# A tuned attention and MLP kernel on one core: small vectors spread on chip, first K and Q columns loaded apart, and the instruction order searched anew

## The chip, the cores and the metric

The kernel runs on one core of a Trainium2 chip. The metric is the device time of one execution in microseconds (us). The core has five engines that run side by side: TensorE (PE; PEld is its weight load), VectorE (DVE), ScalarE (ACT), GpSimd (POOL) and SyncE (SP, which here only issues DMAs). Sixteen DMA engines move data between HBM and on-chip memory.

## The reference, cut to what matters

```python
g = sigmoid((x * gate_w).sum(-1, keepdims=True))      # x: 2048 tokens x 512
a = A(x, wq, wk, wv, wo, beta)   # 32 heads of 16, four segments of 512 tokens:
                                 # causal softmax attention in a segment, plus a memory
                                 # (phi(q) M / phi(q) z) of the segments before,
                                 # mixed per head by sigmoid(beta)
b = (gelu(x @ w_gate) * (x @ w_up)) @ w_down          # 512 -> 1792 -> 512
return g * a + (1 - g) * b
```

Two inputs are tiny: `beta` has 32 values and `gate_w` has 512, all bfloat16.

## The kernel before

The kernel describes its work as tasks with estimated durations and lets a list scheduler, run at build time, put them in order on each engine. A table `BIAS` of priorities, found by search, steers the list. Every engine then executes its list strictly in order.

A segment's attention is a rhythm of 20 steps: TensorE computes scores (lines L730) into four banks of PSUM, ScalarE takes one exponential over 2048 columns (L738), GpSimd masks it (L750), TensorE multiplies by V (L763). In the gaps between scores TensorE does projections and MLP matmuls (L421). The four score banks exist once, so scores n+1 cannot start before exponential n has read scores n.

The head of the kernel, with the parts that changed:

```python
for a in range(2):                                   # x of segment 0, 2 x 256 KB, natural layout
    dma(f"x0_{a}", SP, ..., A_x[0, a * 256:(a + 1) * 256, :] ...)
wdma("wk", SP, wk[:], r4(A_wk), 524288)
wdma("wq", SP, wq[:], r4(A_wq), 524288)
wdma("wv", SP, wv[:], r4(A_wv), 524288)
wdma("beta", ACT, betab[:], A_beta.partition_broadcast(P), 8192)
for g in range(4):                                   # beta again, in another layout
    bsrc = A_beta.rearrange("(t g j) -> g t j", g=4, j=2)[g]
    dma(f"betaT{g}", ACT, lambda g=g: betaT[32 * g:32 * g + 32, :].rearrange("p (t j) -> p t j", j=2),
        lambda bsrc=bsrc: bsrc.partition_broadcast(32), ...)
wdma("gatew", ACT, gatew[:], gate_w.rearrange("(kb p) -> p kb", p=P), 1024, nonc=True)
# ... w_gate, x of segment 1 (DMA transposes), w_up, w_down, wo, all on SP
# warm-up: 10 matmuls on zeros; then x0 is transposed by TensorE in four groups, each into one
# of three work banks of PSUM and copied out from there; then 3 more warming matmuls ("warmE")
```

`partition_broadcast(32)` makes 32 partitions read the same source bytes. So each of the four `betaT` loads is 128 reads of 4 bytes. `betab` is 128 reads of 64 bytes. `gatew` is 512 reads of 2 bytes.

The softmax here doesn't subtract the row's maximum and nothing guards it: scores larger than these inputs give would overflow.

Of the kernel before, what the change touches and what calls it, by code (L numbers as in the profile page):

```python
# [10 lines left out]
BF = mybir.dt.bfloat16  # L11
# [18 lines left out]
BIAS = {  # L30
    "D1": 28, "D2": -81, "D3": -30, "G1": -23, "G2": -26, "G3": 129, "GdT0": 14, "GdT1": 24, "GdT3": -43,
    "Gev1": 11, "K0": 2, "K2": -15, "K3": -12, "Q0": -31, "Q1": 2, "Q2": -21, "Q3": -15, "U0": 55, "U1": 21,
    "U2": -32, "U3": 1, "Um1": 8, "Um2": 42, "Um3": 4, "V1": 13, "V2": -15, "Vev0": -8, "Vev2": 2, "Vev3": 28,
    "den1": -8, "den3": 4, "denp2": 4, "exp1": 4, "exp2": -2, "exsT0": -30, "exsT1": -8, "exsT2": 4, "exsT3":
    -12, "fin1": -20, "fin2": -15, "fin3": -64, "gate2": -4, "gelu1": -8, "gelu2": 13, "gelu3": -6, "gexs0":
    -34, "gexs2": 30, "gts0": -4, "gts2": -28, "gts3": -73, "kp0": 39, "kp1": -9, "kp2": 94, "kp3": 30,
    "msk1": -40, "msk2": 7, "msk3": 6, "mz0": 4, "mz1": 22, "mz2": -64, "mzacc0": 23, "mzacc2": -2, "mzbd0":
    9, "mzbd1": -6, "mzbd2": -19, "norm1": -6, "norm2": -33, "num1": -9, "num3": 10, "nump1": 22, "nump2": 34,
    "nump3": 2, "oTd2": -26, "pkT1": 4, "pkc0": 30, "pkc1": -43, "pke0": -35, "pke2": 4, "pqc2": -8, "pqc3":
    8, "pqe1": -4, "pv0": 21, "pv1": -23, "pvt2": -11, "pvt3": -52, "qk0": 26, "qk3": -12, "x2": 4, "x3": -37  # L40
}
# [68 lines left out]
class Sched:  # L110
# [32 lines left out]
    def schedule(self):  # L143
# [26 lines left out]
        for t in tasks:  # L170
            if npred[t.id] == 0:
                for e in t.alts:
                    ready[e].add(t)
        cur = {e: 0.0 for e in ENGINES}
        bank_free = {b: 0.0 for b in range(self.nbanks)}
# [3 lines left out]
        while len(order) < n:  # L179
# [33 lines left out]
            if t.nbytes:  # L213
                dma_free = max(t.finish + 1.5, dma_free) + t.nbytes / DMA_RATE
                avail = dma_free
# [111 lines left out]
def mm_t(n):  # L327
    return max(0.026, n / 2370.0)
# [19 lines left out]
def _build(es, nc, A_x, A_wq, A_wk, A_wv, A_wo, A_beta, B_w_gate, B_w_up, B_w_down, gate_w, out):  # L348
    def sb(name, shape, dtype=BF):
        return es.enter_context(nc.sbuf_tensor(name, shape, dtype))  # L350
# [30 lines left out]
    exsT = [sb(f"exsT{i}", [P, 16], F32) for i in range(2)]  # L381
    betaT = sb("betaT", [P, 8])
    gexpT = sb("gexpT", [P, 8], F32)
    omgT = sb("omgT", [P, 8], F32)
# [56 lines left out]

    def dma(name, eng, out_ap, in_ap, reads, writes, nbytes, issue=0.7, transpose=False, bias=0.0, sm=None,
            nonc=False):
        sm = sm if sm is not None else sem("d")

        def f(e):
            if transpose:
                return e.dma_start_transpose(out_ap(), in_ap())
            if nonc:
                with nc.allow_non_contiguous_dma(reason="small vector"):  # L450
                    return e.dma_start(out_ap(), in_ap())
            return e.dma_start(out_ap(), in_ap())  # L452
        return task(name, eng, [Instr(f, reads, writes, issue, dma_sem=sm)], bias=bias, nbytes=nbytes)
# [7 lines left out]
    def xdma(s):  # L461
# [12 lines left out]
    task("ident", POOL, [  # L474
        Instr(lambda e: e.memset(ident[:], 0.0), writes=[("c", "ident")], est=0.2),
        Instr(lambda e: e.affine_select(out=ident[:], in_=ident[:], compare_op=ALU.not_equal, fill=1.0, base=0,
# [6 lines left out]
    for a in range(2):  # L483
# [3 lines left out]
            [("hT", 1, 2 * a), ("hT", 1, 2 * a + 1)], 262144, bias=rank[0], issue=0.45)  # L487
    wdma("wk", SP, wk[:], r4(A_wk), 524288)
    wdma("wq", SP, wq[:], r4(A_wq), 524288)
    wdma("wv", SP, wv[:], r4(A_wv), 524288)  # L490
    wdma("beta", ACT, betab[:], A_beta.partition_broadcast(P), 8192)
    for g in range(4):
        bsrc = A_beta.rearrange("(t g j) -> g t j", g=4, j=2)[g]
        rank[0] -= 20.0
        dma(f"betaT{g}", ACT, lambda g=g: betaT[32 * g:32 * g + 32, :].rearrange("p (t j) -> p t j", j=2),
            lambda bsrc=bsrc: bsrc.partition_broadcast(32), [], [("betaT", g)], 1024, nonc=True, bias=rank[0],
            issue=0.5)
    wdma("gatew", ACT, gatew[:], gate_w.rearrange("(kb p) -> p kb", p=P), 1024, nonc=True)
    wdma(("wg", 0), SP, wg[:, :, 0:half], wgr[:, :, 0:half], 917504)
# [8 lines left out]
                             [("P",)], 0.43)], bias=5001.0)  # L508
    for i in range(9):
        gw = Grp(banks)  # L510
        task(f"warm{i}", PE, [Instr(lambda e, gw=gw: e.matmul(gw.f32()[:, :], warm[:, 0:128], warm, start=True,
                                                              stop=True), [wkey], [gw.key], 0.43)],
             grp=gw, bias=5000.0 - i)
    for kb in range(4):
        g = Grp(banks)
        task(f"x0t{kb}", PE, [Instr(lambda e, g=g, kb=kb, a=a: e.transpose(
            g.bf()[:, a * 128:(a + 1) * 128], xin[:, a, kb * 128:(kb + 1) * 128], ident[:, :]),
            [("hT", 1, a), ("c", "ident")], [g.key], mm_t(128)) for a in range(4)], grp=g)
        copy_out(f"x0ev{kb}", g, lambda kb=kb: xT[0][:, kb, :], lambda g=g: g.bf()[:, 0:512], [g.key],
                 [("xT", 0, kb)], 512)  # L520
    task("warmE", PE, [Instr(lambda e: e.matmul(Pb[:, :], warm[:, 0:128], warm, start=True, stop=True), [wkey],
                             [("P",)], 0.3) for _ in range(3)], bias=4.0,
         after=[t for t in S.tasks if t.name == "x0t3"])

    c = [Instr(lambda e: e.memset(maskc[0][:], 0.0), writes=[("c", "mask", 0)], est=0.1)]
# [23 lines left out]
    def exp_task(phase, name, instrs, **kw):  # L549
# [4 lines left out]
        if phase > 0 and name.endswith("_0A0"):  # L554
# [3 lines left out]

    exp_task(0, "gexp", [
        Instr(lambda e: e.activation(gexp[:], betab[:], ACTF.Exp), [("w", "beta")], [("c", "gexp")], 0.25),  # L560
        Instr(lambda e: e.activation(gexpT[:], betaT[:], ACTF.Exp), [("betaT", g) for g in range(4)],
              [("c", "gexpT")], 0.25)])
    task("gmat", DVE, [
        Instr(lambda e: e.tensor_scalar(gexpT[:], gexpT[:], 1.0, None, ALU.add), [("c", "gexpT")],
              [("c", "gexpT")], 0.2),
        Instr(lambda e: e.reciprocal(omgT[:], gexpT[:]), [("c", "gexpT")], [("c", "omgT")], 0.2),
        Instr(lambda e: e.tensor_scalar(gtmp[:], gexp[:], 1.0, None, ALU.add), [("c", "gexp")], [("c", "gtmp")], 0.2),
        Instr(lambda e: e.reciprocal(gtmp[:], gtmp[:]), [("c", "gtmp")], [("c", "gtmp")], 0.2),
        Instr(lambda e: e.tensor_tensor(gmat[:], gexp[:], gtmp[:], ALU.mult), [("c", "gexp"), ("c", "gtmp")],
              [("c", "gmat")], 0.2)])  # L570

    def proj_T(name, s, t, w, wkey, dst, wkeys, even=None):

        g = Grp(banks)
        xs = xT[s % NX]
        pieces(name, g, [mm(g, lambda: g.f32()[:, :], w[:, kb, t * 128:(t + 1) * 128], xs[:, kb, :],
                            [("xT", s % NX, kb), ("w", wkey)], kb == 0, kb == 3, 512) for kb in range(4)], 2)
        if even is not None:
            task(name + "even", ACT, [Instr(lambda e: e.activation(even[0], g.f32()[:, :], ACTF.Copy,
                                                                   scale=maskc[0][:, 0:1]),  # L580
                                            [g.key, ("c", "mask", 0)], [even[1]], act_t(512, ap=True))], grp=g)
        copy_out(name + "ev", g, lambda: dst[:, t, :], lambda: g.f32()[:, :], [g.key], wkeys, 512)

    def phi_task(nm, s, phase, src, skey, dst, dkey, i):
# [12 lines left out]
            Instr(lambda e: e.tensor_tensor(dst[:, t0:t1, :], dst[:, t0:t1, :], ex[:], ALU.add),  # L597
                  dk + [("pex", i)], dk, dve_t(1024, 2))])

    def prep(s):  # L600
# [19 lines left out]
        for tile in range(4):  # L620
# [24 lines left out]
        cross = task(f"exsT{s}", POOL, [Instr(lambda e, g=g, c=c: e.tensor_copy(  # L645
            exsT[sl][32 * g:32 * g + 32, c:16:4], exs[32 * c:32 * c + 32, s4]), [("exs", s), ek], [ek], 0.2)
            for g in range(4) for c in range(4)])
        for ins in cross.alts[POOL]:
# [3 lines left out]
            exsT[sl][:].rearrange("p (o b) -> p o b", o=1).to_broadcast([P, 8, 16]), ALU.mult),  # L652
            [ek, ("c", "omgT")], [("GdT", sl)], 0.3)])
        if s > 0:
            for i in range(2):
# [9 lines left out]
                      0.3),  # L665
                Instr(lambda e: e.reciprocal(nf, nf), [("nd",)], [("nd",)], 0.3),
                Instr(lambda e: e.tensor_tensor(ndsc[:], ndsc[:], Gm[sl][:], ALU.mult), [("nd",), ("Gm", sl)],
# [230 lines left out]
    fins = []  # L898
    sem_out = [sem("so") for _ in range(16)]
    prep(0)  # L900
    memory(0)
# [99 lines left out]
```

## Time and profile before

| | us |
|---|---|
| time, median of 3 runs | 293.34 (293.33 to 293.64) |
| span of the profiled run | 290.8 |
| head: start to first scores | 16.13 |
| middle: first scores to last scores | 260.27 |
| tail: last scores to end | 14.42 |

"First scores" is the start of the first L730 matmul in the timeline. Head, middle and tail, cut at the score matmuls, add up to the span.

The page of the kernel before, first its totals, then forty slices of the span (busy tenths, granted clock in tenths, DMA throughput), then one DMA queue and the chain of waits:

```profile
PE 272.3 (94%) x2150; PEld 114.2 (39%) x2189; DVE 191.3 (66%) x332; ACT 217.5 (75%) x172; POOL 103.0 (35%) x193
...
PE   6699999999999899996799999999999999999995
...
PEclk9899999999999999999799999999999999999999
...
GB/s 88 285 246 342 280 102 2 0 1 2 0 2 72 73 109 38 1 0 20 54 2 0 36 38 36 10 29 2 0 2 0 1 3 0 48 45 38 19 2 72
...
q10 hardware_dynamic: 1248, 0.01, 0.2%
...
PE 79%; DVE 9%; ACT 5%; DMA 3%; issue 2%; POOL 1%; SPq 0%; ACTq 0%
```

TensorE is the engine that bounds: 94% busy, 79% of the chain. But its first two slices (14.5 us) are only 6 tenths busy, and those are warming matmuls in good part; the clock is below full in the second; and in the first slice the DMA engines move 88 GB/s, against 342 later. Queue q10 (the one that ScalarE issues on) carries 1,248 packets for 0.01 MB.

The chain of waits, in order of time (start, length, what):

```profile
2.33 9.81 DMA wq<-in_A_wq_dram
...
12.19 3.17 PE psW L421 x7
```

The windows view of the head (window, its length, busy time and count for PE, PEld, DVE, ACT and POOL, then the granted clock, DMA share, GB/s):

```profile
2.00:4.00 2.00, 2.00 (x6) 0.76 (x5) 0.00 (x0) 0.00 (x0) 1.85 (x4) 1.00 0.38 103
4.00:6.00 2.00, 1.73 (x7) 0.55 (x4) 0.00 (x0) 0.54 (x1) 2.00 (x2) 1.00 0.38 124
12.00:14.00 2.00, 1.81 (x5) 0.71 (x6) 0.80 (x4) 0.96 (x2) 0.00 (x0) 0.55 0.88 282
14.00:16.00 2.00, 2.00 (x7) 0.51 (x5) 0.95 (x2) 0.19 (x1) 0.00 (x0) 0.59 1.07 389
```

About 113 GB/s move from 2 to 6 us, with the DMA engines 38% busy. The clock falls to 0.55 and 0.59 between 12 and 16 us.

The worst place of the middle, in the timeline of TensorE (start, length, instruction, in brackets the idle time before it and what ended it):

```profile
134.64 0.40 PE L730 MATMUL psXALL<-qT,kpad_1 32*128 32x256 bf16 x8 [0.19 <-ACT pt L738]
135.24 0.41 PE L421 MATMUL psW<-mzbd,phq 128*128 128x128 bf16 x4 [0.20 <-DVE otok L677]
137.16 0.39 PE L730 MATMUL psXALL<-qT,kpad_1 32*128 32x512 bf16 x4 [1.51 <-ACT pt L738]
139.61 2.34 PE L421 MATMUL psW<-xT,wu 128*128 128x512 bf16 x5 [2.05 <-DVE otok L677]
```

Here the only matmuls in TensorE's list between two scores are a few small ones (`mzbd,phq`, the memory's numerator), and the next projection waits 2.05 us until VectorE has written `otok` and so freed one of the three work banks.

### The profile page before, as it was taken

How to read it: one execution, taken by the hardware profiler on the slowest of the kernel's cores; microseconds unless marked ns; L12 is line 12 of the kernel's file. 1: busy time of each engine (PE TensorE's matmuls, PEld its weight loads, DVE VectorE, ACT ScalarE, POOL GpSimd, SP SyncE). 2: the span in 40 equal slices, each digit the busy share in tenths (PEclk: the TensorE clock that was granted, in tenths of full speed). 3: DMA queues.
4: the chain of work that ended last, by engine and by line, in shares of the span. 5: the costliest groups of instructions: out<-in, count | busy, mean ns of one | idle time of the engine just before them, and what ended most of it. 6: DMA issues, size and time to landing. Idle time of an engine off the chain costs nothing.

```text
span 290.8 us, 5337 instructions
## 1 busy us (share of the span) xinstructions
PE 272.3 (94%) x2150; PEld 114.2 (39%) x2189; DVE 191.3 (66%) x332; ACT 217.5 (75%) x172; POOL 103.0 (35%) x193
## 2 busy tenths in 40 slices
PE   6699999999999899996799999999999999999995
PEld 2234343343455343432244343344344434533342
DVE  0378898885887947899451926299980767772432
ACT  2377898888998767986668878789787767777722
POOL 8015864344006353343200334366420243343320
PEclk9899999999999999999799999999999999999999
DMA  3999990000005541000200121000000000211002
GB/s 88 285 246 342 280 102 2 0 1 2 0 2 72 73 109 38 1 0 20 54 2 0 36 38 36 10 29 2 0 2 0 1 3 0 48 45 38 19 2 72
DMA packets 29737, 15.30 MB, mean 53 GB/s; under 512 B 21264, under 2 KB 29712, under 8 KB 29712
## 3 DMA queue, kind: packets, MB, share of 16 engines
q1 hardware_dynamic: 28464, 14.95, 22.5%
q8 instruction: 17, 0.28, 0.4%
q10 hardware_dynamic: 1248, 0.01, 0.2%
q14 instruction: 8, 0.07, 0.1%
HBM read 8.14 MB, written 2.10 MB: 35 GB/s over the span
## 4 chain that ended last, share of the span: by engine, by line
PE 79%; DVE 9%; ACT 5%; DMA 3%; issue 2%; POOL 1%; SPq 0%; ACTq 0%
PE psW L421 64%; PE psXALL L730 8%; PE psP L763 6%; ACT pt L738 5%; DMA wq<-in_A_wq_dram 3%; PE psXALL L421 1%; DVE tb L771 1%; DVE kpad_1 L617 1%; DVE hT L861 1%; DVE otok L677 1%; POOL pt L750 1%; DVE kT L597 1%; DVE ost L889 0%; SPq L452 0%; DVE pex L595 0%
## 5 line engine op out<-in xcount | busy, mean ns | idle before, releaser
L738 ACT ACTIVATE pt<-psXALL 128x2048 bf16<-128x2048 f32 x80 | 150.1, 1877 | 42.6 <-PE psXALL L730 27.9
L750 POOL TENSOR_SCALAR_AFFINE_SELECT pt<-pt 128x512 bf16<-128x512 bf16 (+1 forms) x112 | 83.2, 745 | 172.4 <-ACT pt L738 151.7
L421 PE MATMUL psW<-xT,wu 128*128 128x512 bf16 x216 | 52.1, 386 | 2.8 <-DVE otok L677 2.1
L861 DVE TENSOR_TENSOR hT<-psW,hT 128x512 bf16<-128x512 f32 x56 | 37.1, 686 | 26.3 <-PE psW L421 26.1
L421 PE MATMUL psW<-xT,wg 128*128 128x512 bf16 x217 | 50.7, 380 | 0.8 <-ACT hT L840 0.2
L421 PE MATMUL psW<-wd,hT 128*128 128x512 bf16 x203 | 50.5, 380 | 0.5 <-issue 0.2
L771 DVE STREAM_TRANSPOSE tb<-psP 128x512 f32<-128x512 f32 x32 | 22.9, 714 | 31.7 <-PE psP L763 31.4
L421 PEld LDWEIGHTS psW<-xT,wu 128*128 128x128 bf16 x224 | 20.5, 99 | 29.0 <-issue 3.3
L421 PEld LDWEIGHTS psW<-xT,wg 128*128 128x128 bf16 x224 | 20.5, 98 | 25.5 <-issue 1.7
L421 PEld LDWEIGHTS psW<-wd,hT 128*128 128x128 bf16 x210 | 18.8, 98 | 22.4 <-issue 3.3
L763 PE MATMUL psP<-pt,vaug 128*17 128x256 bf16 (+3 forms) x512 | 23.3, 301 | 0.6 <-POOL pt L750 0.6
L840 ACT ACTIVATE hT<-psW 128x512 bf16<-128x512 f32 x28 | 16.4, 597 | 6.7 <-PE psW L421 6.7
L421 PE MATMUL psW<-xT,wq 128*128 128x512 bf16 x59 | 16.3, 397 | 2.6 <-DMA wq<-in_A_wq_dram 2.0
L730 PE MATMUL psXALL<-qT,kpad_1 32*128 32x512 bf16 (+3 forms) x256 | 15.8, 301 | 2.6 <-ACT pt L738 2.6
L421 PE MATMUL psW<-xT,wk 128*128 128x512 bf16 x61 | 16.2, 396 | 0.3 <-DVE sc_1 L785 0.2
L421 PE MATMUL psW<-wv,xT 128*128 128x512 bf16 x61 | 15.7, 381 | 0.3 <-DVE vaug L438 0.2
L438 DVE CAST hT<-psW 128x512 bf16<-128x512 f32 x20 | 13.5, 683 | 3.8 <-PE psW L421 3.4
L730 PE MATMUL psXALL<-qT,kpad_0 32*128 32x512 bf16 (+3 forms) x256 | 15.8, 301 | 0.1
L763 PEld LDWEIGHTS psP<-pt,vaug 128*17 128x17 bf16 x512 | 10.0, 89 | 14.0 <-issue 5.9
L645 POOL COPY exsT<-exs 32x4 f32<-32x4 f32 x64 | 14.1, 220 | 3.7
L421 PE MATMUL psW<-wo,oT 128*128 128x512 bf16 x54 | 14.6, 380 | 0.6 <-issue 0.3
L829 ACT ACTIVATE hT<-hT 128x2048 bf16<-128x2048 bf16 (+2 forms) x6 | 12.7, 2185 | 0.0
(93 smaller groups left out, 242.5 us busy)
## 6 DMA issues: line engine op xcount, KB each, us to landing
out_dram<-ost SPq DMA_DIRECT2D x16, 128.0 KB, 1.7
wg<-in_B_w_gate_dram SPq DMA_DIRECT2D x2, 896.0 KB, 13.1
wu<-in_B_w_up_dram SPq DMA_DIRECT2D x2, 896.0 KB, 7.0
wd<-in_B_w_down_dram SPq DMA_DIRECT2D x1, 1792.0 KB, 13.0
hT<-in_A_x_dram SPq DMA_DIRECT2D x2, 256.0 KB, 5.0
wk<-in_A_wk_dram SPq DMA_DIRECT2D x1, 512.0 KB, 7.2
wq<-in_A_wq_dram SPq DMA_DIRECT2D x1, 512.0 KB, 9.8
wv<-in_A_wv_dram SPq DMA_DIRECT2D x1, 512.0 KB, 12.5
```

Source lines behind the costliest of these rows:

```text
L421: return Instr(lambda e: e.matmul(view(), lhsT, rhs, start=first, stop=last), reads=reads, writes=[fkey if fkey is not None else g.key], e ...
L438: alts[DVE] = [Instr(lambda e: e.tensor_copy(dst(), src()), reads=reads, writes=writes, est=dve_t(n))]
L597: Instr(lambda e: e.tensor_tensor(dst[:, t0:t1, :], dst[:, t0:t1, :], ex[:], ALU.add), dk + [("pex", i)], dk, dve_t(1024, 2))])
L645: cross = task(f"exsT{s}", POOL, [Instr(lambda e, g=g, c=c: e.tensor_copy(exsT[sl][32 * g:32 * g + 32, c:16:4], exs[32 * c:32 * c + 32, s4 ...
L730: instrs.append(Instr(lambda e, t=t, g=g, j=j, kb=kb, ncol=ncol, c0=c0: e.matmul(X[g][:, c0:c0 + ncol], kpad[j][sl][32 * g:32 * g + 32, t, ...
L738: prev_exp[0] = exp_task(s, f"exp{s}_{t}{name}", [Instr(lambda e: e.activation(PT[slot][:], XALL[:, :].rearrange("p (g c) -> p g c", g=4), ...
L750: minstrs.append(Instr(lambda e, view=view, pat=pat: e.affine_select(out=view, in_=view, compare_op=ALU.is_ge, fill=0.0, base=0, pattern=p ...
L763: instrs.append(Instr(lambda e, q=q, kb=kb, slot=slot, c0=c0, h=h: e.matmul(Pb[32 * q:32 * q + 17, 128 * kb:512], Vaug[sl][:, kb, h, :], P ...
L771: task(f"pvt{s}_{t}_{j}", DVE, [Instr(lambda e: e.transpose(Tb[i2][:, j, :], Pb[:, :]), [("P",)], [("Tb", i2, j)], dve_t(512))])
L829: t = task(f"gelu{s}_{f0}", ACT, [Instr(lambda e, hv=hv: e.activation(hv, hv, ACTF.Gelu_apprx_tanh), hk, hk, act_t(512 * n, False) + (0.0 ...
L840: lambda e, g=g, ft=ft, s=s: e.activation(hT[s % 2][:, ft, :], g.f32()[:, :], ACTF.Gelu_apprx_tanh),
L861: task(f"Um{s}_{ft}", DVE, [Instr(lambda e, g=g, ft=ft: e.tensor_tensor(hT[sl][:, ft, :], g.f32()[:, :], hT[sl][:, ft, :], ALU.mult), [g.k ...
```

## The change

Five things change together:

1. `beta` is loaded once (the 128-partition broadcast, now on SP behind the weights), and the second layout is made on chip by four GpSimd copies. `gate_w` is loaded as 4 rows of 256 bytes and transposed by TensorE. ScalarE issues no DMA any more.
2. `wk` and `wq` come in two parts: 128 columns of each first, then the other 384.
3. x0 is transposed into the four score banks instead of three work banks, and the second warm-up is dropped.
4. Some durations in the scheduler are corrected (for instance a reciprocal from 0.3 to 0.95).
5. The table of priorities is searched anew.

```diff
-    "D1": 28, "D2": -81, ...                          # whole table
+    "D0": 18, "D1": -562, ...
-            dma_free = max(t.finish + 1.5, dma_free) + ...
+            dma_free = max(t.finish + 2.2, dma_free) + ...
-    wdma("wk", SP, wk[:], r4(A_wk), 524288)
-    wdma("wq", SP, wq[:], r4(A_wq), 524288)
+    for c0, c1 in ((0, 128), (128, 512)):
+        for key, w, src in (("wk", wk, A_wk), ("wq", wq, A_wq)):
+            wdma((key, c0 > 0), SP, w[:, :, c0:c1], r4(src)[:, :, c0:c1], ...)
     wdma("wv", SP, wv[:], r4(A_wv), 524288)
-    wdma("beta", ACT, betab[:], A_beta.partition_broadcast(P), 8192)
-    for g in range(4):
-        ... dma(f"betaT{g}", ACT, ...)
-    wdma("gatew", ACT, gatew[:], gate_w.rearrange("(kb p) -> p kb", p=P), 1024, nonc=True)
+    wdma("gwrow", SP, gwrow[:], gate_w.rearrange("(kb p) -> kb p", p=P), 16384)
+    wdma("beta", SP, betab[:], A_beta.partition_broadcast(P), 65536)
-    for i in range(9):                                # warming matmuls
+    for i in range(8):
-        task(f"x0t{kb}", PE, [... e.transpose(g.bf()[:, ...], xin[...], ident) ...], grp=g)
+        task(f"x0t{kb}", PE, [... e.transpose(XB[:, kb * 1024 + ...], xin[...], ident) ...])
-    task("warmE", PE, [...] * 3)
+    omg = task("omg", POOL, [... e.tensor_copy(omgT[32 * g:32 * g + 32, :] ..., gtmp[...] ...) for g in range(4)])
# [cuts: the rest of the table, other durations, the gate row's transpose and copy]
```

The emitted order of the DMAs on SP is x0, wq first part, wk first part, wq rest, wv, wk rest, four DMA transposes of x1, beta, gate rows, then the MLP weights.

## The prediction

> **What bounds it.** TensorE: the page gives it 94% of the 290.8 us span, and the chain of waits runs 79% through it. Matmuls counted in the issue order at the trace's start-to-start 0.216 us (128x512) make about 251 us of work. The timeline shows a rhythm: each 2048-wide exponential (1.88 us on ScalarE) needs new scores; from scores to scores is at least 2.52 us, 2.59 us with ten projection matmuls between. Time is lost in three places:
> 1. Head: the first scores start at 16.13 us, after only 14 projection matmuls. The chain has 9.81 us of waiting for wq, which lands at 12.14. Then the clock falls: 0.55 and 0.59 in windows 12-14 and 14-16.
> 2. Middle, first to last scores, 260.3 us: at 132-142 us slots hold 0.5 to 1.5 us of TensorE work, then comes a 2.05 us wait for VectorE's otok; the clock halves again at 138.5. Smaller holes lie near 33 us (masks behind gate copies on GpSimd) and 95-99 us (VectorE).
> 3. Tail: 14.4 us, 10.9 of it matmuls.
>
> **Head.** Queue q10 carries 1,248 packets for 0.01 MB, pieces of 2 to 64 bytes, beside x0, wk and wq; in windows 2-4 and 4-6 us only 103 and 124 GB/s move. "DMA: Bandwidth & Descriptors" (Trainium skill; "Rules for kernel authors") says a strided last dimension becomes one descriptor per element; these packets agree. All but one beta broadcast (128 packets) and 4 gate rows go, and those follow the weights. ScalarE loses 4.6 us of DMA issuing; its table load moves from 5.5 to about 1 us. wk and wq first bring 128 columns: 2 x 512 packets of 256 B; the transposes' 256 B packets move at about 1,000 per us at 20 us, so about 1 us. x0 then lands at about 6 instead of 7.2 us, both pieces at 7.5 to 8.5. Four score banks spare x0's transposes a 0.24 us wait. 14 projection matmuls again precede the first scores (3.0 us plus 0.6 for the copy): first scores at 11.5 to 13.5 us, estimate 12.3; gain 3.8 us, all critical. Added: two DMA issues of 0.5 us on SP, a 4-column transpose, four tiny GpSimd copies.
>
> **Middle.** The new order fills the hole: counting each slot as the larger of 2.52 us and its work plus 0.2 us, the old order needs 253.6 us (took 260.3), the new 250.7. Slots under 1.9 us of work fall from three to one. I expect 3 to 4 us over that count instead of 6.7: about 254, gain 6. Tail unchanged.
>
> Sum: 9.8 us less, nearly all critical: **283.6 us**, 8 in 10 between 280.5 and 288.0. Chances: faster by over 2% 0.86, within 2% 0.13, slower 0.01.
>
> **Shows in:** start of the first scores (12.3) and first wide exponential (12.8); wait for first wq/wk columns under 2 us, none later for wv or gate weights over 1 us; clock; no TensorE gap over 1 us in the middle; first to last scores about 254.
>
> **What would make it wrong.** Beta and gate rows queue behind four x1 transposes on SP; in the old trace the first took 5.65 us to issue on a full queue. If beta lands after about 17 us, ScalarE stands (its exponential precedes the fourth wide one), and TensorE with it; likewise the gate row (needed at 21 us). The clock may halve at about 8.8 us if TensorE idles too long before ("TensorE: Matmul & The Clock Gate", Part 1, states a window of about 3.4 us; here both half-clock stretches lasted 3.41 us): up to 1.7 us. New VectorE waits.

## The result

| us | before | after | difference | predicted |
|---|---|---|---|---|
| time, median of 4 runs each | 293.33 | 280.96 (280.66 to 281.27) | -12.37 | -9.8 |
| head | 16.13 | 9.46 | -6.67 | -3.8 |
| middle | 260.27 | 255.08 | -5.19 | -6 |
| tail | 14.42 | 14.43 | 0.0 | 0 |

The ratio is 0.9576 (95% interval 0.956 to 0.9593). All ratios here are the mean time of one kernel's fast runs over that of the other's in the same rounds, so not quite the ratio of the medians quoted. The time lies inside the stated range (280.5 to 288.0), near its fast end. Head, middle and tail are read from one profiled execution of each kernel and add up to 11.9 us; the kernel before took 292.53 us in its profiled run, 0.8 less than its median, and the kernel after 280.67, 0.3 less, which makes the other 0.5 us.

The page of the kernel after:

```profile
PE 267.8 (96%) x2148; PEld 113.4 (41%) x2186; DVE 192.1 (69%) x334; ACT 215.4 (77%) x168; POOL 103.8 (37%) x197
...
PE   8999999999999999999999999899999999999995
...
PEclk9999999999999999999999999999999999999999
...
GB/s 194 200 382 359 206 59 2 0 4 0 0 58 57 40 75 59 19 40 38 2 0 19 59 0 2 36 22 2 21 0 0 0 4 2 37 77 22 18 2 75
...
PE 87%; DVE 5%; ACT 4%; issue 2%; POOL 1%; ACTq 0%; DVEq 0%
```

The head of TensorE's row is full from the first slices, the clock stays at full speed until the end, the first two slices move 194 and 200 GB/s instead of 88 and 285, q10 is gone, and the chain runs 87% through TensorE.

The chain of waits of the head has no DMA in it any more:

```profile
1.87 3.41 PE psW L509 x8
5.29 0.98 PE psXALL L514 x16
...
6.33 3.19 PE psW L424 x14
9.52 0.33 PE psXALL L737 x4
```

L509 are the warming matmuls, L514 the transposes of x0, L424 the projections, L737 the first scores. In the trace's landing records x0 is complete at 4.31 us (before: 7.16), the first part of wq at 6.20, that of wk at 6.71. The windows view:

```profile
2.00:4.00 2.00, 2.00 (x6) 0.76 (x5) 0.00 (x0) 0.29 (x2) 1.85 (x4) 1.00 0.98 292
4.00:6.00 2.00, 2.00 (x19) 1.22 (x17) 0.14 (x1) 0.37 (x1) 2.00 (x2) 1.00 0.77 214
```

In 2 to 4 us 292 GB/s move where 103 did. The middle's worst place, in the same stretch of the algorithm:

```profile
121.78 0.41 PE L424 MATMUL psW<-mzbd,phq 128*128 128x128 bf16 x4 [0.19 <-DVE otok L684]
122.22 0.40 PE L737 MATMUL psXALL<-qT,kpad_1 32*128 32x384 bf16 x8
...
123.20 0.41 PE L424 MATMUL psW<-mzbd,phq 128*128 128x128 bf16 x4
123.45 1.46 PE L424 MATMUL psW<-xT,wk 128*128 128x512 bf16 x6
124.84 0.40 PE L737 MATMUL psXALL<-qT,kpad_1 32*128 32x256 bf16 x8
```

The small `mzbd,phq` matmuls now have projections (`wk`, `wu`) between and behind them. The longest waits of TensorE, before and then after (total, times, longest), show the same:

```profile
PE psW L421 <- DVE otok L677: 3.4, 3, 2.1
PE psXALL L730 <- ACT pt L738: 2.6, 5, 1.5
PE psW L421 <- DMA wq<-in_A_wq_dram: 2.0, 1, 2.0
PE psW L516 <- DMA hT<-in_A_x_dram: 1.5, 1, 1.5
```

```profile
PE psW L424 <- issue: 2.7, 17, 0.2
PE psP L505 <- DVE pt L482: 1.3, 1, 1.3
PE psW L424 <- DVE ost L896: 0.7, 1, 0.7
```

After the change the longest wait of TensorE, apart from the 1.3 us before its very first instruction, is 0.7 us.

### The profile page after: what moved, and what is told of

Read it like the earlier page. It is cut to its first block, busy times and chain, and to the rows that moved or that the text cites. A ratio compares the mean times of both kernels' runs of the same rounds, so it can differ in the third digit from the quotient of the medians.

```text
span 279.0 us, 5322 instructions
## 1 busy us (share of the span) xinstructions
PE 267.8 (96%) x2148; PEld 113.4 (41%) x2186; DVE 192.1 (69%) x334; ACT 215.4 (77%) x168; POOL 103.8 (37%) x197
## 4 chain that ended last, share of the span: by engine, by line
PE 87%; DVE 5%; ACT 4%; issue 2%; POOL 1%; ACTq 0%; DVEq 0%
PE psW L424 68%; PE psXALL L737 9%; PE psP L770 6%; ACT pt L745 4%; DVE kpad_1 L624 2%; PE psXALL L424 1%; PE psW L509 1%; DVE hT L868 1%; POOL pt L757 1%; DVE hT L441 0%; DVE oT L798 0%; DVE otok L684 0%; DVE obf L794 0%; PE psXALL L514 0%; DVE ott L796 0%
## 5 line engine op out<-in xcount | busy, mean ns | idle before, releaser
L424 PE MATMUL psW<-xT,wu 128*128 128x512 bf16 x217 | 51.4, 380 | 1.4 <-issue 0.6
L424 PE MATMUL psW<-xT,wg 128*128 128x512 bf16 x215 | 50.6, 380 | 1.3 <-issue 0.8
L424 PE MATMUL psW<-wd,hT 128*128 128x512 bf16 x201 | 50.1, 380 | 1.0 <-issue 0.8
L424 PEld LDWEIGHTS psW<-xT,wu 128*128 128x128 bf16 x224 | 20.3, 97 | 27.8 <-DVE hT L868 2.9
L424 PEld LDWEIGHTS psW<-xT,wg 128*128 128x128 bf16 x224 | 20.4, 98 | 26.2 <-issue 2.1
L424 PEld LDWEIGHTS psW<-wd,hT 128*128 128x128 bf16 x210 | 18.6, 98 | 22.4 <-issue 4.0
L424 PE MATMUL psW<-xT,wk 128*128 128x512 bf16 x60 | 15.9, 379 | 0.7 <-issue 0.3
L737 PE MATMUL psXALL<-qT,kpad_0 32*128 32x512 bf16 (+3 forms) x256 | 15.8, 301 | 0.4 <-ACT exs L641 0.2
L737 PE MATMUL psXALL<-qT,kpad_1 32*128 32x512 bf16 (+3 forms) x256 | 15.8, 301 | 0.3 <-ACT pt L745 0.3
L424 PE MATMUL psW<-xT,wq 128*128 128x512 bf16 x61 | 15.3, 379 | 0.5 <-DVE mzacc L710 0.2
L424 PE MATMUL psW<-wo,oT 128*128 128x512 bf16 x56 | 14.6, 380 | 0.9 <-DVE ost L896 0.7
L424 PE MATMUL psW<-wv,xT 128*128 128x512 bf16 x62 | 15.3, 380 | 0.1
L652 POOL COPY exsT<-exs 32x4 f32<-32x4 f32 x64 | 13.5, 212 | 3.6
## 6 DMA issues: line engine op xcount, KB each, us to landing
wu<-in_B_w_up_dram SPq DMA_DIRECT2D x2, 896.0 KB, 10.5
```

The lines of the kernel that those rows point to most:

```text
L424: return Instr(lambda e: e.matmul(view(), lhsT, rhs, start=first, stop=last), reads=reads, writes=[fkey if fkey is not None else g.key], e ...
L652: cross = task(f"exsT{s}", POOL, [Instr(lambda e, g=g, c=c: e.tensor_copy(exsT[sl][32 * g:32 * g + 32, c:16:4], exs[32 * c:32 * c + 32, s4 ...
L737: instrs.append(Instr(lambda e, t=t, g=g, j=j, kb=kb, ncol=ncol, c0=c0: e.matmul(X[g][:, c0:c0 + ncol], kpad[j][sl][32 * g:32 * g + 32, t, ...
```

## The experiments

Two questions stood: what made the head gain 6.67 us where 3.8 had been foreseen, and how much of the whole belongs to the new order. Twelve kernels were run, each with three timed rounds against the kernel before. "First scores" is read from each profiled run. Times of different groups of runs were taken on different occasions; the kernel before had medians from 292.7 to 293.8 us there.

| run | time, us | ratio to before (95%) | head | middle | tail |
|---|---|---|---|---|---|
| before | 293.33 | 1 | 16.13 | 260.27 | 14.42 |
| e1 fewer packets | 289.35 | 0.9878 (0.985 to 0.9906) | 12.22 | 260.47 | 14.43 |
| e2 spread only | 297.98 | 1.0158 (1.0104 to 1.0213) | 12.02 | 269.68 | 13.36 |
| e3 split only | 291.77 | 0.9957 (0.993 to 0.9984) | 14.92 | 261.00 | 14.41 |
| e4 warm wait | 293.46 | 1.0011 (0.9986 to 1.0036) | 16.02 | 260.41 | 14.42 |
| e6 new priorities only | 290.82 | 0.9937 (0.987 to 1.0004) | 15.72 | 258.22 | 14.42 |
| after | 280.96 | 0.9576 (0.956 to 0.9593) | 9.46 | 255.08 | 14.43 |
| e5 after, old priorities | 290.98 | 0.9922 (0.9876 to 0.9968) | 9.29 | 260.29 | 19.60 |
| e7 after, 512 beta reads back | 283.20 | 0.9667 (0.9648 to 0.9687) | 11.99 | 255.06 | 14.39 |
| e8 after, work banks | 281.05 | 0.9583 (0.9539 to 0.9627) | 9.81 | 255.03 | 14.43 |
| e9 after, whole wq and wk | 282.58 | 0.9627 (0.9578 to 0.9675) | 10.97 | 255.06 | 14.43 |
| e10 after, 512 gate reads, ACT | 280.90 | 0.9563 (0.9522 to 0.9604) | 9.39 | 254.84 | 14.40 |
| e11 after, 512 gate reads, SP | 280.68 | 0.9561 (0.9521 to 0.9601) | 9.39 | 255.06 | 14.39 |
| e12 after, 512 reads apart | 280.83 | 0.9552 (0.9494 to 0.9611) | 9.42 | 255.13 | 14.40 |

### The head, first round: packets or amount?

Theory P said that the many tiny packets on ScalarE's queue hold back x0 and the weights. Rival O said that only the amount of data ahead of the first scores counts.

**e1, fewer packets.** The five small loads stay where they are but read contiguous values: the results are wrong (relative error 0.05), all engines execute the same instructions in the same order.

```diff
-        bsrc = A_beta.rearrange("(t g j) -> g t j", g=4, j=2)[g]      # 128 pieces of 4 bytes per load
+        bsrc = A_beta.rearrange("(g j) -> g j", g=4)[g]               # 32 pieces of 16 bytes per load
-    wdma("gatew", ACT, gatew[:], gate_w.rearrange("(kb p) -> p kb", p=P), ...)   # 512 of 2 bytes
+    wdma("gatew", ACT, gatew[:], gate_w.rearrange("(p kb) -> p kb", p=P), ...)   # 128 of 8 bytes
```

> The kernel before, every instruction in its old place, but the five small loads read contiguous values (wrong numbers on purpose): 1,248 packets become 384. Theory P (many tiny packets on the second queue hold back x0, wk and wq): the windows 2-6 us move about 250 GB/s instead of about 113, wq lands near 9.5 instead of 12.1 us, first scores near 12.5 instead of 16.1 us, time about 3.5 us lower (289.8). Rival O (only the amount of data ahead of the first scores counts; the head was slow for other reasons): wq within 0.5 us of 12.1, time within 0.5 us of before.

First scores came at 12.22 us, 3.91 us earlier, and the time fell by 1.2%. The Q projections started at 9.95 instead of 12.19 us. 241 GB/s moved from 4 to 6 us, but only 71 from 2 to 4 us, so P had the rate half right. Middle and tail did not move: what the head gains reaches the end in full. P is supported; O alone is out. But e1 also cut the reads that fall on the same 64 bytes of beta, from 640 to 256, so it cannot tell the number of packets from what they read.

**e3, split only.** Into the kernel before, only the split of wk and wq.

```diff
-    wdma("wk", SP, wk[:], r4(A_wk), 524288)
-    wdma("wq", SP, wq[:], r4(A_wq), 524288)
+    for c0, c1 in ((0, 128), (128, 512)): ...          # as in the change
```

> The kernel before with only wk and wq split into 128 and 384 columns; TensorE, VectorE, ScalarE and GpSimd orders are unchanged. Theory O (amount ahead of the first scores): first pieces of both land near 9 us although x0 still lands at 7.2, first scores near 12.5 us, time about 3.5 us lower. Theory P alone: the gain is small, since the small packets still slow everything: first scores after 15 us, time less than 1 us lower.

First scores came at 14.92 us: 1.2 us gained, between the two forecasts. The timeline shows why so little: the old order of TensorE asks for the second K tile and for V before the first scores.

```profile
10.03 1.04 PE L421 MATMUL psW<-xT,wq 128*128 128x512 bf16 x4 [0.62 <-DMA wq<-in_A_wq_dram]
12.37 1.04 PE L421 MATMUL psW<-xT,wk 128*128 128x512 bf16 x4 [1.30 <-DMA wk<-in_A_wk_dram]
14.40 0.59 PE L421 MATMUL psW<-wv,xT 128*128 128x512 bf16 x2 [0.99 <-DMA wv<-in_A_wv_dram]
14.92 0.40 PE L731 MATMUL psXALL<-qT,kpad 32*128 32x512 bf16 x4
```

The first K and Q columns are used at 8.39 and 10.03 us, but then TensorE waits for the rest of wk and for wv. An earlier piece pays only if the order behind it can live on that piece.

**e4, warm wait.** The prediction counted the half clock at 12.2 us as lost time. Here TensorE is kept busy while it waits for wq, by 12 instead of 3 warming matmuls.

```diff
-    task("warmE", PE, [Instr(... matmul(Pb, warm, ...), [("P",)], 0.3) for _ in range(3)], ...)
+    task("warmE", PE, [Instr(... matmul(Pb, warm, ...), [("P",)], 0.075) for _ in range(12)], ...)
```

> The kernel before with 12 instead of 3 warming matmuls after the x0 transposes, so that TensorE is busy while it waits for wq; all orders else unchanged. If the half clock from 12.2 to 15.6 us is caused by that wait, it goes, the ten matmuls before the first scores take 2.2 instead of 4.0 us, first scores near 14.4 us, time about 1.7 us lower (291.6). If the clock falls anyway, or the start of the scores waits for ScalarE or VectorE, less than 0.5 us.

The clock stayed full at the head and the ten matmuls ran at full speed, but the forecast 1.7 us did not come (ratio 1.0011):

```profile
12.22 1.04 PE L421 MATMUL psW<-xT,wq 128*128 128x512 bf16 x4 [0.31 <-DMA wq<-in_A_wq_dram]
13.10 1.03 PE L421 MATMUL psW<-xT,wk 128*128 128x512 bf16 x4
15.50 0.59 PE L421 MATMUL psW<-wv,xT 128*128 128x512 bf16 x2 [1.37 <-DMA wv<-in_A_wv_dram]
16.02 0.39 PE L730 MATMUL psXALL<-qT,kpad 32*128 32x512 bf16 x4
```

The matmuls that used to fill the time up to 15.5 us slowly now fill it quickly, and then TensorE stands 1.37 us for wv, which lands at 15.4 us in the kernel before too. The half clock at the head was in the shadow of the next DMA. The cause (an idle TensorE) was right; its price was zero.

**e7, beta reads back.** The mirror of e1: the kernel after, with four loads of 128 pieces of 4 bytes that nobody uses, issued while ScalarE is free.

```diff
+            em.emit_stream(ACT, 1)                     # table load and its first use
+            for g in range(4):
+                bsrc = A_beta.rearrange("(t g j) -> g t j", g=4, j=2)[g]
+                e.dma_start(spare[32 * g:32 * g + 32, :].rearrange("p (t j) -> p t j", j=2),
+                            bsrc.partition_broadcast(32)).then_inc(sem_spare, 16)
+            em.emit_stream(ACT, None, 1)               # the rest
```

> The kernel after with four unused loads of beta in 4-byte pieces (512 packets) issued by ScalarE right after its table load, when it has nothing to do until 5.6 us; all else unchanged. Theory P: x0 and the first pieces come 1 to 2 us later, first scores at 10.5 to 11.5 instead of 9.5 us, time 1 to 2 us higher (282 to 283). Theory O: first scores within 0.3 us of 9.5, time within 0.4 us of 281.0.

First scores moved from 9.46 to 11.99 us and the time by 2.2 us: 512 packets that carry 2 KB cost 0.8% of the kernel. The first parts of wq and wk landed at 7.92 and 8.34 instead of 6.20 and 6.71 us, and the rest of wq, which the last six matmuls before the first scores wait for, at 10.54 instead of 7.89. The delay is larger than P had forecast (10.5 to 11.5 us).

### The head, second round: which property of the packets?

So far this fits the prediction's reason, one packet per element. The next three runs tried to take it apart.

**e10 and e11.** One unused load of the gate row in 512 pieces of 2 bytes, on ScalarE's queue (e10) or on the weights' own queue behind x0 (e11).

```diff
+            e.dma_start(spare[:], gate_w.rearrange("(kb p) -> p kb", p=P)).then_inc(sem_spare, 16)
```

> The kernel after with one unused load of the gate row in 512 pieces of 2 bytes, issued by ScalarE after its table load. If the number of small packets on the other queue counts, not their bytes or the number of loads: like the run with four loads and 512 packets, first scores near 12.0 us, time near 283.2. If four separate loads made that delay: first scores before 10.3 us.

> The same load of 512 pieces of 2 bytes, but issued by SP on the weights' own queue, behind x0 and ahead of wq. If every small packet holds its engine for about 100 ns wherever it is queued (estimate: 13 us of idle engine time beside 78 small packets in one us of the trace before gives up to 170 ns each): 512 packets over 16 engines cost about 3 us more before wq, first scores near 12 to 12.5 us, time 2.5 to 3 us higher. If the harm comes from alternating between two queues: only the 0.5 us of issuing and under 0.3 us of transfer, first scores near 10.0 us, time about 0.6 higher.

Neither cost time: first scores at 9.39 us in both, times of 280.90 and 280.68 us against 280.96. The packets did take room: in e10, 158 GB/s moved from 3 to 4 us where the kernel after moved 325, and x0 was complete at 5.24 instead of 4.31 us, so that its transposes waited for it:

```profile
5.29 0.95 PE L520 MATMUL psXALL<-ident,hT 128*128 128x128 bf16 x14 [0.35 <-DMA hT<-in_A_x_dram]
```

But the first parts of wq and wk landed no later than in the kernel after (5.75 and 6.20 us in e10, 5.85 and 6.28 in e11), and the scores did not move. Every expectation that came from "small packets are slow" missed, and "two queues alternate" could not explain e7 against e10. The theory as predicted had fallen. What was left to differ between e7 and e10 was the number of loads, the size of the pieces (4 against 2 bytes), and where they read: e7 reads the same 64 bytes of HBM 512 times over in small parts, e10 reads 512 different elements.

**e12, the same reads, apart.** e7 with only the source changed: the pieces come from 128 rows of x. Number of loads, packets, bytes and the time of issue are equal.

```diff
-                bsrc = A_beta.rearrange("(t g j) -> g t j", g=4, j=2)[g]
+                bsrc = A_x[0, 32 * g:32 * g + 32, 0:32].rearrange("p (t g j) -> g p t j", g=4, j=2)[g]
-                            bsrc.partition_broadcast(32)).then_inc(sem_spare, 16)
+                            bsrc).then_inc(sem_spare, 16)
```

> The kernel with four unused loads of 512 4-byte pieces (first scores 11.99, 283.2 us) again, with one thing changed: the pieces come from 128 different rows of x instead of from the same 64 bytes of beta for every partition. Number, size and time of issue are equal. Theory R (many reads of the same few bytes of HBM are what is slow, near 100 per us for all engines together, and the weights' packets wait behind them): the 512 packets drain in under 2.5 us, first scores at 9.4 to 9.9 us, time 280.7 to 281.4. Rival N (four separate loads of 4-byte pieces are slow from anywhere): first scores near 12.0, time near 283.2.

First scores at 9.42 us, time 280.83 us: the delay is gone. The windows view of e7, then of e12 (clock, DMA share and GB/s are the last three columns):

```profile
2.00:4.00 2.00, 2.00 (x6) 0.76 (x5) 0.00 (x0) 0.28 (x2) 1.85 (x4) 1.00 0.68 178
4.00:6.00 2.00, 2.00 (x17) 1.21 (x16) 0.11 (x1) 0.34 (x1) 2.00 (x2) 1.00 0.38 104
6.00:8.00 2.00, 0.30 (x6) 0.12 (x3) 0.74 (x2) 0.75 (x2) 1.06 (x4) 1.00 0.57 123
```

```profile
2.00:4.00 2.00, 2.00 (x6) 0.76 (x5) 0.00 (x0) 0.29 (x2) 1.85 (x4) 1.00 0.99 279
4.00:6.00 2.00, 2.00 (x18) 1.23 (x16) 0.14 (x1) 0.36 (x1) 2.00 (x2) 1.00 0.92 229
6.00:8.00 2.00, 1.98 (x13) 0.93 (x11) 0.71 (x2) 0.93 (x3) 1.07 (x4) 1.00 1.06 364
```

Between 4 and 8 us, e7 moves 104 and 123 GB/s with its DMA engines busy 0.38 and 0.57 of the time; e12 moves 229 and 364. (Where records overlap a share can pass 1.00.) The DMA view of a window counts the packets of ScalarE's queue, first e7 from 3 to 8 us, then e12 from 2.5 to 5.5 us:

```profile
q10 hardware_dynamic: 485, 0.00, 4.6%
```

```profile
q10 hardware_dynamic: 568, 0.00, 10.6%
```

485 packets in 5 us are 97 per us for all sixteen engines together; 568 in 3 us are 189 per us, with the weights flowing beside them. (Each kernel has 576 packets on this queue, the 512 reads and 64 more, 16 for each load.) In the kernel before, the same view counts 425 such packets from 4 to 9 us, 85 per us. While they wait, the packets of the weights behind them on the same DMA engines wait too. That the wait is at the memory for the repeated bytes is the reading of these runs; where in the memory path it arises, no run shows. A rival stays open: e12 changes the tensor together with the repetition, and no run read beta's bytes only once or broadcast other bytes, so something peculiar to where beta lies is not ruled out. A small region read often is not enough by itself: e10's 512 reads fall on the 1 KB of the gate row.

The change leaves one such load, the broadcast of beta to 128 partitions: 128 reads of the same 64 bytes. In e5 (below; the kernel after with the old table) it runs beside weights that had been issued long before: w_gate stands behind it on the queue from 5.94 us on, and the 128 reads start between 8.38 and 10.74 us. The windows view of e5:

```profile
8.00:9.00 1.00, 1.00 (x6) 0.39 (x4) 0.55 (x1) 0.89 (x2) 0.00 (x0) 1.00 1.05 294
9.00:10.00 1.00, 0.99 (x8) 0.34 (x7) 0.83 (x3) 0.60 (x2) 0.00 (x0) 1.00 0.31 75
11.00:12.00 1.00, 1.00 (x9) 0.34 (x11) 0.71 (x2) 0.79 (x2) 0.26 (x1) 1.00 1.05 405
```

75 GB/s move among the reads, 405 after them. In the kernel after, the same 128 reads start between 12.06 and 13.35 us, where nothing waits for what follows. There they cannot be shown to hold anything up: w_gate was issued only at 11.90 us, and its first packet starts 1.06 us later, as x0's first packet starts 1.09 us after its issue.

**e9, whole weights first.** How much is the split worth once the repeated reads are gone? The first loads bring all 512 columns of wq and wk; the order of all engines is held.

```diff
-            wdma((key, c0 > 0), SP, w[:, :, c0:c1], r4(src)[:, :, c0:c1], ...)
+            wdma((key, c0 > 0), SP, w[:] if c0 == 0 else spare[...], r4(src) if c0 == 0 else A_wo[0:128, 0:64], ...)
```

> The kernel after with the first loads of wq and wk bringing all 512 columns and the two later loads replaced by a 16 KB load that nobody reads; order of all compute engines equal. Theory: with the small packets gone the split is worth the time that 0.75 MB takes, at about 330 GB/s 2.3 us: wk usable near 9.0 instead of 6.8 us, first scores at 11 to 12 instead of 9.5 us, time about 2 us higher (283). Rival (small packets were everything, the split is worth little): first scores before 10.2, time under 281.7.

First scores at 10.97 us, 1.51 us later, and the time at 282.58 us. The split is worth 1.5 us in the new order (wk was used from 8.28, not from the 9.0 expected) and 1.2 us in the old one (e3).

**e8, work banks.** x0's transposes back in the three work banks.

```diff
-        task(f"x0t{kb}", PE, [... e.transpose(XB[:, kb * 1024 + ...], ...) ...])
+        g = Grp(banks)
+        task(f"x0t{kb}", PE, [... e.transpose(g.bf()[:, ...], ...) ...], grp=g)
```

> The kernel after with x0's transposes back in the three work banks; orders else equal. The fourth group of transposes must wait for an evacuation (0.24 us in the kernel before), the last xT piece comes 0.3 to 0.6 us later, but the third and fourth matmul pairs are what needs it: first scores 0.2 to 0.5 us later, time up to 0.5 us higher. Rival: no difference (under 0.2 us), since wk's first piece lands at 6.7 us, after the evacuations.

First scores 0.35 us later in the trace, as the first forecast had it; the time, 281.05 us, cannot be told from 280.96.

### The order

**e2, spread only.** Part 1 of the change alone, with the old table.

```diff
# from the change: gwrow and beta on SP, gate row transposed on chip, omgT made by GpSimd copies; old BIAS, wk and wq whole
```

> The kernel before with only beta and gate rows spread on chip and their loads moved behind the weights; old priorities. Head: as theory P has it, wq lands at 9 us and the first scores start near 11.5 us, a gain of 4 to 5 us. But the list order changes everywhere (13 instead of 7 slots between scores hold less than 2.3 us of TensorE work), the count of slots gives 261.9 instead of 253.6 us in the middle, 7.1 instead of 10.9 us of work in the tail: middle about 266, tail about 10.5. So the sum is about 288 plus 2.5: 290.5, most of the head's gain given back. If the order did not matter the time would be 289 or less.

The head gained 4.11 us, and the kernel became 1.6% slower than before: the middle took 269.68 us. The task graph had changed a little at its start, and the same table then led the list to another order everywhere. The count of slots (each slot between two scores taken as the larger of 2.52 us and its TensorE work plus 0.2 us) had forecast 262 us without waits, 8 more than before; it gave the direction, and the sum of 290.5 us was too kind by 7.5.

**e5, old priorities.** The kernel after with the old table.

```diff
-BIAS = { new table }
+BIAS = { old table }
```

> The kernel after with the old table of priorities. Theory that the new search and not the head is what saves the middle: first scores stay near 9.5 us, but slots hold as little as 0.47 us of TensorE work again and the tail has 16.1 us of work instead of 10.9; middle about 257, tail about 19.5: time about 288.5, that is 7 to 8 us slower than after. Rival (the new durations in the scheduler and the earlier head suffice): within 2 us of 281.

The head kept its gain (9.29 us), but the middle took 260.29 and the tail 19.60 us, with 16.1 us of matmuls left over for it: 290.98 us, 10.0 us more than after and 2.5 more than expected. Nearly all of the structural gain is given back without a new search.

**e6, new priorities only.** The kernel before with the new table.

```diff
-BIAS = { old table }
+BIAS = { new table }
```

> The kernel before with only the new table of priorities. If the table is good by itself: the middle falls from 260.3 to about 255 and the time to about 288. If a table fits only the graph it was searched for: the count of slots gives 253.3 us, hardly under the 253.6 of before, with nine short slots, the middle stays near 259 and the time within 2 us of 293.

290.82 us with an interval of the ratio that just reaches 1: the middle fell by 2 us to 258.22, not by 5. The middle is near the second forecast (259), the time 0.2 us outside it: a table fits, in the main, the graph it was searched for. e5 and after differ in the table alone, so the 10.0 us between them are the table's, on the new graph and durations. What the corrected durations are worth by themselves stays open: no run changed them alone (e6 has the old ones).

## Why the prediction was right, and where it was not

- **TensorE bounds, with the rhythm of scores and exponential.** Right. The median slot from scores to scores takes 2.6 us in both kernels; what changed is the filling of the slots, and the head.
- **The head's reason.** The prediction said that "a strided last dimension becomes one descriptor per element; these packets agree", and that taking them off q10 brings the early loads sooner. The queue was the right one, and the gate row's 512 packets of 2 bytes are one per element, as the Trainium skill ("DMA: Bandwidth & Descriptors", section "Rules for kernel authors") describes them (the small pieces of beta hold two elements each). But the property was wrong. 512 packets of 2 bytes (e10, e11) or of 4 bytes from different rows (e12) cost no time that can be told, though those of e10 held up x0 by 0.9 us, unseen in the time; 512 packets of 4 bytes from the same 64 bytes cost 2.5 us (e7). The change took the small packets and the repeated reads out of the early loads together, so the gain came although the property named was the wrong one: that part is luck. The same page, section "Issuing engines are not separate DMA queues", says that DMAs of all queues run on the same 16 engines and interleave. e7 agrees: loads on ScalarE's queue delayed the weights on SP's by 1.6 to 2.7 us against the kernel after.
- **The head's size.** The term that was mis-sized is the arrival of the data: "x0 then lands at about 6", "both pieces at 7.5 to 8.5". The runs show 4.31 us for x0 and 6.20 and 6.71 us for the pieces, because 292 GB/s move from 2 to 4 us once the repeated reads are gone (without the split, in e2, x0 is complete at 4.24 us). From the first Q matmul to the first scores 3.13 us pass, not 3.6. Together (2.37 and 0.47 us) that is the 2.8 us by which the head beat its forecast.
- **The clock.** The prediction listed the half clock among the head's losses and allowed up to 1.7 us for a new one. The Trainium skill ("TensorE: Matmul & The Clock Gate", Part 1) states a window of about 3.4 us; the granted clock in the trace before was 0.5 for 3.41 us from 12.21 and again from 138.51 us, which agrees. e4 shows that the first of these cost nothing. In the kernel after no half clock appears before the last microsecond.
- **Four score banks.** 0.24 us expected, 0.35 us in one trace of e8, and no difference in time that can be told.
- **The middle.** 254 expected, 255.08 measured. The hole at 132 to 142 us is gone, and after its first instruction no wait of TensorE exceeds 0.7 us. e2 and e5 show that this belongs to the new order: with the old table the middle takes 5.2 us longer and the tail another 5.2, and the same structure is only 0.8% faster than the kernel before.
- **Beta and gate rows behind x1.** Named as the main risk; it did not come true. Beta landed at 13.70 us (used at 14.35), and the gate rows were used at 17.25 us (the trace has no landing of theirs). The first DMA transpose took 2.18 us to issue, not 5.65; why, no run isolates.
- **The tail.** Unchanged, as predicted.

What is still open: x0 is complete at 4.31 us, but the transposes start at 5.08 us, when the warming matmuls end. Whether fewer of them would help, or would bring the half clock into the projections, was not tried; the wk piece at 6.71 us would limit the gain. None of the runs beat the kernel after by more than its own spread.

## What to carry to other kernels

Before blaming many small DMA packets, ask what they read: a broadcast load that reads the same few bytes for every partition can hold up the loads beside and behind it, as 512 reads from the same 64 bytes of beta did here, so load such a vector once and spread it on chip, or put the broadcast where nothing waits behind it. A stall or a slow clock has a price only if the next thing to arrive is not later anyway; a run that removes it, as e4 did, is the only proof. And in a kernel whose order is searched, a change to the graph and the search belong together: judge a structural part with the order held fixed, since with the old table a gain of 4 us at the head came out as a loss of 1.6%.

## What the Trainium skill lacked or had wrong

- "DMA: Bandwidth & Descriptors" (section "Rules for kernel authors") lets a source repeat, as in a broadcast, and names no cost of reading the same bytes. Here 512 reads of 4 bytes from the same 64 bytes drained at about 97 per us over all engines, and the first parts of wq and wk landed 1.9 to 2.0 us later than with as many reads from different rows (e7 against e12).
- The same table advises against a strided last dimension because it becomes one descriptor per element. True as to the count; but 512 such 2-byte packets on a queue that carried the weights cost no measurable time here (e11: 280.68 against 280.96 us).
